# Two attention blocks on one core: K transposed in pairs of 64-row tiles on TensorE instead of partly by DMA, P transposed into score banks, Q and O copied four heads at a time

## The chip, the cores and the metric

The kernel runs on one core of one Trainium2 chip. The metric is the device time of one execution in microseconds (us). The kernel before has three timed runs: 896.97, 900.49 and 900.94 us, median 900.49. A separate, profiled execution gives the profile; its span, from the first to the last instruction, is 898.5 us.

## What is computed

Two independent blocks, A and B, of the same form; their outputs stand side by side in the last dimension.

```python
B, Sq, D, H, Sk, Dh = 16, 64, 640, 32, 512, 128      # all bfloat16
q = (x @ wq).reshape(B, Sq, H, Dh).transpose(0, 2, 1, 3)
scores = einsum("bhqd,bhkd->bhqk", q, k_cache) * (Dh ** -0.5)
p = softmax(scores, axis=-1)
o = einsum("bhqk,bhkd->bhqd", p, v_cache)
y = o.transpose(0, 2, 1, 3).reshape(B, Sq, H * Dh) @ wo
```

The keys and the values of a block are 16 x 32 x 512 x 128, 67 MB each. Four such tensors are 268 MB, by far most of what is read.

## The kernel before, in words

**Tiles.** A step is one head of a pair of batches: 2 x 64 query rows fill the 128 partitions. Two steps make a macro, m. There are 512 steps and 256 macros. Eight macros (16 heads) of one batch pair make a group, of which there are 32; eight groups, one for each batch pair, make a pass, over one half of the heads of one block. A chunk of K or V is four heads of a batch pair: two loads (one for each batch, j) of 512 KB. Two macros use one chunk of each.

**A macro's work.** Its operations have two-letter names in the code:

- KX (L457) transposes K on TensorE. K lies in `kn_ring` with the rows of two heads stacked (64 partitions each, eight rows of K in each partition). For one batch j there are eight 128x128 transposes, into one PSUM bank (7).
- KE (L466) copies that bank, 1024 elements wide, to `ktp_ring` on VectorE, and separates the two heads on the way.
- QP2 (L475) projects Q for both heads, 2 x 5 matmuls into half of bank 1. QE2 (L484) scales and copies it on ScalarE, 256 columns.
- SM (L496) forms the scores of one step as two matmuls, one for each batch, on the two column halves of the array (`tile_position`), 512 columns each. Scores have four banks, 2 to 5, used in turn.
- MX (L505, VectorE) takes the negated maximum; EX (L511, ScalarE) the exponential with the row sums; RC2 (L517, VectorE) the reciprocals of two steps; NM (L525, GpSimd) the normalised P.
- TR2 (L534) transposes P of both heads, eight 128x128 transposes into bank 6. It is copied to `pT_ring` by VectorE (TE2, L541) or by ScalarE (TA2, L546): by ScalarE for the even macros, unless the group four macros on is loaded transposed.
- PV2 (L558) multiplies with V, 16 matmuls of 64 columns into the other half of bank 1. OE2 (L566, ScalarE) copies O, 256 columns.
- OP2 (L574) adds the first 512 of 640 output columns into bank 0, over 16 heads. OX (L584) does the other 128 columns for a whole group at once, 16 matmuls into the first score bank (PSUM bank 2), in the last macro of the group. In the very last group it is split in two, so that only the last four heads' share is left for the end. The sums of the first half of the heads are kept (OVP, OXP, ScalarE); those of the second are added to them (OVF, OXF, VectorE) and stored.

**K by transposing DMA.** For 11 of the 32 groups (`TGROUPS`), K of the second batch (j = 1) does not go through KX and KE. One transposing load for each group (LDKT, L651) brings all 16 heads to `kd_sb`, from where SM reads it. Those groups have half the KX and KE.

**Order.** Nothing is scheduled at run time. `Cfg` holds a template for each engine: which operation of which macro (relative to the period) at what time of a period of two macros. The lists are unrolled over all macros; each engine works through its own in order, with semaphore waits worked out from what each operation reads and writes. A PSUM bank counts as one resource, so whoever writes a bank waits for its last reader. The loads are put into one list for SP by due times and ring slots (`SLOT_NS` and `DMA_NS` are the planner's estimates); a load into a ring waits for the last reader of the slot, and all loads behind it in the queue wait as well. Rings: four chunks of K, five of V, six slots each of wq and wo (a pass needs four of each).

Of the kernel before, what the change touches and what calls it, by code (L numbers as in the profile page):

```python
# [14 lines left out]
class Cfg:  # L15
    G = 4
    HH = 16
    NKB = 4
    NW = 6
    TGROUPS = (4, 6, 11, 13, 15, 19, 21, 23, 27, 29, 31)  # L20
    TLEAD = 1.0
    NVB = 5
    XLEAD = 1.5
    NQ = 3
    NKT = 5
# [3 lines left out]
    NO = 9  # L29
    NR = 8  # L30
    NS = 4
    PERIOD = 6.7
    PE_T = (("SM", 0, 0, 0.0), ("SM", 0, 1, 0.21), ("SM", 1, 0, 0.43), ("SM", 1, 1, 0.64), ("KX", 2, 1, 0.98),
# [3 lines left out]
    ACT_T = (("EX", 0, 0, 1.13), ("OE2", -3, 0, 2.1), ("EX", 0, 1, 2.49), ("TA2", -2, 0, 3.15), ("QE2", 3, 0, 4.0),  # L37
             ("EX", 1, 0, 4.4), ("OXP", -3, 0, 5.2), ("OE2", -2, 0, 5.34), ("EX", 1, 1, 5.73), ("OVP", -3, 0, 6.4),
             ("QE2", 4, 0, 6.65), ("ST", -3, 0, 6.68))
    DVE_T = (("MX", 0, 0, 0.44), ("MX", 0, 1, 1.06), ("RC2", -1, 0, 1.66), ("KE", 2, 1, 1.68), ("MX", 1, 0, 2.3),  # L40
             ("TE2", -2, 0, 2.6), ("RC2", 0, 0, 3.3), ("KE", 3, 1, 3.43), ("MX", 1, 1, 4.1), ("KE", 3, 0, 4.87),
             ("OXF", -3, 0, 5.3), ("OVF", -3, 0, 5.5), ("TE2", -1, 0, 5.79), ("KE", 4, 0, 6.4))
    POOL_T = (("NM", -1, 0, 1.95), ("NM", -1, 1, 2.8), ("NM", 0, 0, 4.2), ("NM", 0, 1, 5.05))
    TAIL_SPLIT = 2
    SLOT_NS = 3400.0
    DMA_NS = dict(LDK=3100.0, LDKT=9600.0, LDV=3100.0, LDWQ=3900.0, LDWO=4300.0, LDX=700.0)


class Op:
# [3 lines left out]
    def __init__(self, eng, kind, idx, reads=(), writes=(), dur=0.0, ts=None, aux=None):  # L53
        self.eng = eng
        self.kind = kind
        self.idx = idx
        self.reads = tuple(reads)
        self.writes = tuple(writes)
        self.sem = None
        self.count = None  # L60
        self.deps = []
        self.waits = []
        self.dur = dur
        self.ts = ts
        self.aux = aux
        self.dma = kind in ("LDK", "LDKT", "LDV", "LDX", "LDWQ", "LDWO", "ST")


def build_plan(dims, cfg):
# [28 lines left out]
    def by_dma(m, j=1):  # L98
        return j == 1 and m // MPG in cfg.TGROUPS

    tstart = [m for m in range(0, NMAC, MPG) if by_dma(m)]

# [3 lines left out]
    def kslot(m, j):  # L106
        return (4 * (m // 2) + (j if m % 2 == 0 else 3 - j)) % cfg.NKT

    def on_act(m):
        return m % 2 == 0 and not by_dma(min(m + 4, NMAC - 1))  # L110

    def make_op(kind, m, sub, ts):
        g0, g1 = 2 * m, 2 * m + 1
        if kind in ("KX", "KE") and by_dma(m, sub):
            return None
        ps_, bp, grp, h0 = step_info(g0)
        c = g0 // G
        if kind == "KX":
            return mk("pe", "KX", (m, sub), [("kn", c % cfg.NKB, g0 % G), ("kn", c % cfg.NKB, g1 % G), ("ident",)],
                      [("KTB",)], ts)  # L120
        if kind == "KE":
            return mk("dve", "KE", (m, sub), [], [("KTB",), ("ktp", kslot(m, sub))], ts)
# [11 lines left out]
        if kind == "QE2":  # L134
            return mk("act", "QE2", m, [], [("QOB",), ("qT", m % cfg.NQ)], ts)
        if kind == "SM":
            kt = [("ktp", kslot(m, 0)), ("kd",) if by_dma(m) else ("ktp", kslot(m, 1))]
            return mk("pe", "SM", (m, sub), [("qT", m % cfg.NQ)] + kt, [("SB", (2 * m + sub) % cfg.NS)], ts)
        if kind == "RC2":
            return mk("dve", "RC2", m, [("rowsum", r0), ("rowsum", r1)], [("recip", r0), ("recip", r1)], ts)  # L140
        if kind == "TR2":
            return mk("pe", "TR2", m, [("pn", g0 % cfg.NPN), ("pn", g1 % cfg.NPN), ("ident",)], [("PTB",)], ts)
        if kind in ("TE2", "TA2"):
            if (kind == "TA2") != on_act(m):
                return None
            return mk("dve" if kind == "TE2" else "act", kind, m, [], [("PTB",), ("pT", m % cfg.NT)], ts)
# [3 lines left out]
        if kind == "OE2":  # L150
            return mk("act", "OE2", m, [], [("QOB",), ("oT", m % cfg.NO)], ts)
        if kind == "OP2":
            return mk("pe", "OP2", m, [("oT", m % cfg.NO), ("wo", wslot(ps_, h0 // G))], [("OUTB",)], ts)
        lo = grp * MPG
        last = h0 + 2 == SPB
        if kind == "OX":
            hi = m + 1
            if grp == NGRP - 1 and h0 + 6 == SPB:
                pass
            elif not last:  # L160
                return None
            elif grp == NGRP - 1:
                lo = m - 1
            return mk("pe", "OX", m, [("oT", i % cfg.NO) for i in range(lo, hi)]
                      + [("wo", wslot(ps_, i)) for i in sorted({(2 * i % SPB) // G for i in range(lo, hi)})],
                      [("SB", 0)], ts, aux=(lo, hi))
        if not last:
            return None
        if kind in ("OVP", "OXP") and ps_ % NHALF == 0:
            return mk("act", kind, m, [], [("OUTB",) if kind == "OVP" else ("SB", 0), ("outp", bp, kind[1])], ts,  # L170
                      aux=grp)
        if kind in ("OVF", "OXF") and ps_ % NHALF == 1:
            return mk("dve", kind, m, [("outp", bp, kind[1])],
                      [("OUTB",) if kind == "OVF" else ("SB", 0), ("out_sb", kind[1])], ts, aux=grp)
# [40 lines left out]
    def tload(m):  # L215
        return at["SM", m, 0] - cfg.TLEAD

    for blk in range(NBLK):
        for lo, hi in ((0, 1), (1, 2), (2, 4), (4, NBP)) if blk == 0 else ((0, 4), (4, NBP)):
            first = at["QP2", blk * NHALF * MPP + lo * MPG, 0]  # L220
            ready = NEG if blk == 0 else at["QP2", (blk * NHALF - 1) * MPP + hi * MPG - 1, 0]
            due = [tload(m) + 0.003 for m in tstart if ready < tload(m) < first - 4]
            add(ready, due[-1] if due else first - cfg.XLEAD, first, -1, "LDX", (blk, lo),
# [10 lines left out]
    for i, m in enumerate(tstart):  # L234
        ready = NEG if i == 0 else at["SM", tstart[i - 1] + MPG - 1, 1]
        add(ready, tload(m), at["SM", m, 0], 2, "LDKT", m, [("kd",)], (m, 1), cfg.DMA_NS["LDKT"])

    for c in range(NCHUNK):
        m0 = MPC * c
        for kind, ring, n_ring, cons, tb in (("LDK", "kn", cfg.NKB, "KX", 2), ("LDV", "v", cfg.NVB, "PV2", 2.5)):  # L240
# [5 lines left out]
            for pi, (piece, j, hlo, hhi) in enumerate(chunk_pieces(c)):  # L246
                if kind == "LDK" and by_dma(m0, j):
                    continue
# [18 lines left out]
    def sem_key(op):  # L267
        if op.kind == "LDKT":
            return ("d_kd",)
# [28 lines left out]
    for op in sorted(all_ops, key=lambda o: (o.ts, ENGINES.index(o.eng))):  # L298
# [6 lines left out]
        for res in op.writes:  # L305
# [3 lines left out]
            for rd in readers.get(res, ()):  # L309
# [7 lines left out]
                NPASS=NPASS, counts=counts, KT=KT, by_dma=by_dma, wslot=wslot, kslot=kslot)  # L317
# [54 lines left out]
def mha_kernel(nc, blocks, out, cfg=None):  # L372
# [17 lines left out]
    by_dma, wslot, kslot = info["by_dma"], info["wslot"], info["kslot"]  # L390
# [14 lines left out]
    with contextlib.ExitStack() as es:  # L405
# [11 lines left out]
        kd_sb = sb("kd_sb", [128, 8, HH * 64], BF16)  # L417
        ktp_ring = sb("ktp_ring", [128, NKT, 2, SK], BF16)
        qT_ring = sb("qT_ring", [128, NQ, 2, 128], BF16)
# [3 lines left out]
        oT_ring = sb("oT_ring", [128, NO, 2, 128], BF16)  # L423
# [15 lines left out]
        pt_ps_flat = ps[:, PT_BANK, :].bitcast(BF16)  # L439
        pt_ps = pt_ps_flat.rearrange("p (s t q) -> p s t q", s=2, t=4)  # L440
        q_ps = ps[:, QO_BANK, 0:256]
        o_ps = ps[:, QO_BANK, 256:512]
        kt_ps_flat = ps[:, KT_BANK, :].bitcast(BF16)
        kt_ps = kt_ps_flat.rearrange("p (t s) -> p t s", t=8)
# [3 lines left out]

        ox_ps = ps[:, S_BANK0, 0:N1]

        def em_KX(e, op):
            m, j = op.idx
# [3 lines left out]
            for t8 in range(8):  # L456
                ins = e.transpose(kt_ps[:, t8, :], kn_ring[:, c % NKB, j, hp, t8, :], ident[:, :])  # L457
                first = first or ins
                last = ins
            return first, last  # L460

        def em_KE(e, op):
            m, j = op.idx
            src = kt_ps_flat.rearrange("p (t hs pp) -> p t hs pp", t=8, hs=2)
            dst = ktp_ring[:, kslot(m, j)].rearrange("p hs (t pp) -> p t hs pp", t=8)
            ins = e.tensor_copy(dst, src)  # L466
            return ins, ins

        def em_QP2(e, op):
            m = op.idx  # L470
            first = last = None
            for sub in range(2):
                blk, bp, grp, ps_, hh = step_info(2 * m + sub)
                for kt in range(KT):
                    ins = e.matmul(q_ps[:, sub * 128:(sub + 1) * 128],  # L475
# [6 lines left out]
        def em_QE2(e, op):  # L482
            m = op.idx
            ins = e.activation(qT_ring[:, m % NQ].rearrange("p s q -> p (s q)"), q_ps, ACTF.Copy, scale=scale)  # L484
            return ins, ins

        def em_SM(e, op):
            m, sub = op.idx
            first = last = None
            for j in range(2):  # L490
                if by_dma(m, j):
                    hh = (2 * m + sub) % SPB
                    kt = kd_sb[:, :, 64 * hh:64 * hh + 64]
                else:
                    kt = ktp_ring[:, kslot(m, j), sub, :]
                ins = e.matmul(s_bank(2 * m + sub)[64 * j:64 * j + 64, :], qT_ring[:, m % NQ, sub, 64 * j:64 * j + 64],  # L496
                               kt, start=True, stop=True, tile_position=(0, 64 * j))
# [30 lines left out]
        def em_TR2(e, op):  # L528
            m = op.idx
            first = last = None  # L530
            for sub in range(2):
                g = 2 * m + sub
                for t in range(4):
                    ins = e.transpose(pt_ps[:, sub, t, :], pn_ring[:, g % NPN, t * 128:(t + 1) * 128], ident[:, :])  # L534
# [223 lines left out]
```

## Time and profile before

| what | value |
|---|---|
| median of three runs | 900.49 us |
| the profiled execution's span | 898.5 us |
| granted TensorE clock, mean | 0.996 |
| first score matmul starts (L496) | 18.9 us |
| last K load issued (L664) | 864.8 us |
| moved by DMA | 296.81 MB, mean 330 GB/s |
| transposing loads of K (L651) | 11, of 13.5 to 15.5 us in SP's queue |
| PE waited for loads of K and V, in total | 23.2 us, of which 8.6 in one wait at the start |
| SP waited for a free K slot | 75.0 us in 79 waits |
| DVE idle, waiting for KX | 67.2 us |

The span leaves out 2.0 us of the median, what lies around it and the difference between executions; no device time of the profiled execution by itself is listed. In the profile PE is TensorE's matmuls, PEld its weight loads, DVE VectorE, ACT ScalarE, POOL GpSimd, SPq the queue that issues the loads. Lengths of matmuls on PE overlap, since they are pipelined: what one costs is read from starts, not from lengths. A line like `L457 PE MATMUL ps<-ident,kn_ring 128*128 128x128 bf16 x8` is a group of eight matmuls of code line 457, with the array's rows and columns in use, then the moving operand's shape.

### The profile page before, as it was taken

To read this page: it belongs to the slowest core of one execution; us is meant where nothing else is said; L and a number is where in the kernel's file an instruction comes from. 1 tells how busy PE (TensorE), PEld (TensorE's weight loads), DVE (VectorE), ACT (ScalarE), POOL (GpSimd) and SP (SyncE) were. 2 spreads that over 40 slices of the span, in tenths; PEclk is the share of its full clock that TensorE was granted. 3 is DMA by queue.
4 is the path that set the end of the run, shared out by engine and by line. 5 is a ranking of instruction groups with operands and counts; after the bars stand their busy time and mean duration, and the time that the engine had idled before them with its cause. 6 is when DMAs were issued, how large, how long until landed. Compare 5 with 4: busy or idle time off the path is not lost.

```text
span 898.5 us, 33204 instructions
## 1 busy us (share of the span) xinstructions
PE 857.5 (95%) x14016; PEld 691.1 (77%) x14144; DVE 746.6 (83%) x1398; ACT 628.0 (70%) x1651; POOL 413.8 (46%) x518
## 2 busy tenths in 40 slices
PE   4999989999999999999998998999999999999997
PEld 3777777878888877878786787778778777787875
DVE  2888878888888888888887887888888798888896
ACT  1776766777777777767676776777777676776774
POOL 0544444445444454544444444445454444545453
PEclk9999999999999999999999999999999999999999
DMA  9999999999999999999999999999999999999992
GB/s 304 336 340 365 318 272 365 295 361 365 363 366 368 286 361 322 319 369 270 364 361 368 367 260 365 309 324 366 294 363 363 367 370 284 367 286 365 315 333 77
DMA packets 315172, 296.81 MB, mean 330 GB/s; under 512 B 109200, under 2 KB 260752, under 8 KB 315024
## 3 DMA queue, kind: packets, MB, share of 16 engines
q1 hardware_dynamic: 312720, 292.06, 106.3%
q10 hardware_dynamic: 2304, 2.62, 0.9%
q8 instruction: 111, 1.82, 0.9%
q14 instruction: 37, 0.30, 0.1%
HBM read 266.34 MB, written 2.62 MB: 299 GB/s over the span
## 4 chain that ended last, share of the span: by engine, by line
PE 78%; DMA 9%; SPq 7%; DVE 3%; issue 1%; ACT 1%; DVEq 0%; ACTq 0%
PE ps L457 20%; PE ps L475 14%; PE ps L496 12%; PE ps L558 11%; PE ps L534 10%; PE ps L574 9%; DMA kn_ring<-in_B_k_cache_dram 5%; DMA kn_ring<-in_A_k_cache_dram 4%; SPq L651 3%; PE ps L584 3%; SPq L644 2%; DVE ktp_ring L466 1%; SPq L664 1%; DMA wq_sb<-in_A_wq_dram 1%; DVE negmax L505 1%
## 5 line engine op out<-in xcount | busy, mean ns | idle before, releaser
L525 POOL TENSOR_SCALAR pn_ring<-p_ring,recip 128x512 bf16<-128x512 bf16 x512 | 413.1, 843 | 476.1 <-DVE recip L517 475.7
L511 ACT ACTIVATE p_ring<-ps,negmax 128x512 bf16<-128x512 f32 x512 | 350.1, 684 | 100.0 <-DVE negmax L505 100.0
L466 DVE COPY ktp_ring<-ps 128x1024 bf16<-128x1024 bf16 x424 | 290.0, 684 | 82.1 <-PE ps L457 67.2
L505 DVE TENSOR_REDUCE negmax<-ps 128x1 f32<-128x512 f32 x512 | 337.3, 680 | 15.2 <-PE ps L496 4.9
L457 PEld LDWEIGHTS ps<-ident,kn_ring 128*128 128x128 bf16 x3392 | 205.3, 98 | 108.5 <-issue 46.5
L457 PE MATMUL ps<-ident,kn_ring 128*128 128x128 bf16 x3392 | 263.6, 221 | 21.1 <-DMA kn_ring<-in_A_k_cache_dram 11.8
L475 PE MATMUL ps<-xT_sb,wq_sb 128*128 128x128 bf16 x2560 | 187.8, 221 | 1.3 <-DMA wq_sb<-in_A_wq_dram 0.6
L558 PE MATMUL ps<-pT_ring,v_ring 128*128 128x64 bf16 x4096 | 162.0, 193 | 8.6 <-DMA v_ring<-in_B_v_cache_dram 3.1
L475 PEld LDWEIGHTS ps<-xT_sb,wq_sb 128*128 128x128 bf16 x2560 | 154.4, 99 | 16.9 <-ACT oT_ring L566 15.8
L558 PEld LDWEIGHTS ps<-pT_ring,v_ring 128*128 128x128 bf16 x4096 | 141.9, 98 | 28.5 <-issue 26.5
L484 ACT ACTIVATE qT_ring<-ps 128x256 bf16<-128x256 f32 x256 | 98.3, 384 | 86.1 <-PE ps L475 86.0
L534 PE MATMUL ps<-ident,pn_ring 128*128 128x128 bf16 x2048 | 156.4, 219 | 0.0
L566 ACT ACTIVATE oT_ring<-ps 128x256 bf16<-128x256 f32 x256 | 97.6, 381 | 75.3 <-PE ps L558 68.1
L541 DVE COPY pT_ring<-ps 128x1024 bf16<-128x1024 bf16 x174 | 119.5, 687 | 35.5 <-PE ps L534 35.5
L496 PE MATMUL ps<-ktp_ring,qT_ring 128*64 128x512 bf16 x848 | 137.3, 391 | 0.0
L574 PE MATMUL ps<-wo_sb,oT_ring 128*128 128x512 bf16 x384 | 124.5, 379 | 6.8
L534 PEld LDWEIGHTS ps<-ident,pn_ring 128*128 128x128 bf16 x2048 | 118.5, 98 | 0.0
L511 ACT ACTIVATION_READ_ACCUMULATOR p_ring<-ps,negmax 128x1 f32 x512 | 103.1, 201 | 0.0
L546 ACT ACTIVATE pT_ring<-ps 128x1024 bf16<-128x1024 bf16 x82 | 84.0, 1024 | 0.0
L496 PEld LDWEIGHTS ps<-ktp_ring,qT_ring 128*64 128x64 bf16 x848 | 47.1, 110 | 41.0 <-issue 2.1
L517 DVE RECIPROCAL recip<-rowsum 128x2 f32<-128x2 f32 x256 | 40.9, 160 | 14.7 <-ACT p_ring L511 14.6
L496 PE MATMUL ps<-kd_sb,qT_ring 128*64 128x512 bf16 x176 | 47.0, 390 | 0.0
(15 smaller groups left out, 152.0 us busy)
## 6 DMA issues: line engine op xcount, KB each, us to landing
v_ring<-in_A_v_cache_dram SPq DMA_DIRECT2D x128, 512.0 KB, 9.9
v_ring<-in_B_v_cache_dram SPq DMA_DIRECT2D x126, 512.0 KB, 9.8
kn_ring<-in_A_k_cache_dram SPq DMA_DIRECT2D x108, 512.0 KB, 9.4
kn_ring<-in_B_k_cache_dram SPq DMA_DIRECT2D x103, 512.0 KB, 9.3
wq_sb<-in_A_wq_dram SPq DMA_DIRECT2D x8, 640.0 KB, 9.9
wo_sb<-in_A_wo_dram SPq DMA_DIRECT2D x8, 640.0 KB, 10.7
wq_sb<-in_B_wq_dram SPq DMA_DIRECT2D x8, 640.0 KB, 9.7
wo_sb<-in_B_wo_dram SPq DMA_DIRECT2D x8, 640.0 KB, 10.3
```

Source lines behind the costliest of these rows:

```text
L457: ins = e.transpose(kt_ps[:, t8, :], kn_ring[:, c % NKB, j, hp, t8, :], ident[:, :])
L466: ins = e.tensor_copy(dst, src)
L475: ins = e.matmul(q_ps[:, sub * 128:(sub + 1) * 128], wq_sb[:, wslot(ps_, hh // G), kt, (hh % G) * DH:(hh % G + 1) * DH], xT_sb[:, kt, bp * ...
L484: ins = e.activation(qT_ring[:, m % NQ].rearrange("p s q -> p (s q)"), q_ps, ACTF.Copy, scale=scale)
L496: ins = e.matmul(s_bank(2 * m + sub)[64 * j:64 * j + 64, :], qT_ring[:, m % NQ, sub, 64 * j:64 * j + 64], kt, start=True, stop=True, tile_ ...
L505: ins = e.reduce_max(negmax[:, r:r + 1], s_bank(g), axis=AX.X, negate=True)
L511: ins = e.activation(p_ring[:, g % NP, :], s_bank(g), ACTF.Exp, bias=negmax[:, r:r + 1], scale=1.0, accum_out=rowsum[:, r:r + 1])
L525: ins = e.tensor_scalar(dst, src, recip[:, r:r + 1], 1.0, ALU.mult, ALU.mult)
L534: ins = e.transpose(pt_ps[:, sub, t, :], pn_ring[:, g % NPN, t * 128:(t + 1) * 128], ident[:, :])
L541: ins = e.tensor_copy(pT_ring[:, m % NT].rearrange("p s t q -> p (s t q)"), pt_ps_flat)
L558: ins = e.matmul(o_ps[:, col:col + 64], v_ring[:, c % NVB, j, gi, t, :], pT_ring[:, m % NT, sub, t, 64 * j:64 * j + 64], start=(t == 0), s ...
L574: ins = e.matmul(out_ps, oT_ring[:, m % NO, sub, :], wo_sb[:, wslot(ps_, hh // G), hh % G, 0:N0], start=(hh == 0), stop=(hh == SPB - 1))
```

## The change

- **KX** now handles a whole macro: both batches, 32 transposes instead of 2 x 8. Each takes 64 rows (one head) and an identity of 64 columns. The first 64 rows go to bank 6, the other 64 to bank 7, in turn. KE copies both banks at once, 2048 elements, without rearranging. `ktp_ring` has two slots, each of a macro, in place of five of half a macro.
- **No K by transposing DMA**: `TGROUPS`, LDKT and `kd_sb` are gone, and all of K comes by plain loads. The ring of K has five chunks and that of V six.
- **TR2** writes P into the first of the four score banks for even macros and into the second for odd ones; ScalarE copies the even ones, VectorE the odd ones. **OX** uses the third of the four, and is no longer split in the last group.
- **Q and O**: the two macros of a period write Q of four heads into the whole of bank 1, which QE4 copies at once (512 columns); then O of four heads, which OE4 copies at once.
- New templates for all engines, with PV2 one macro earlier (offsets -2 and -1 in place of -3 and -2), and new planner estimates.

```diff
-    NKB = 4
+    NKB = 5
-    TGROUPS = (4, 6, 11, 13, 15, 19, 21, 23, 27, 29, 31)
-    NVB = 5
+    NVB = 6
-    NQ = 3
-    NKT = 5
+    NQ = 2
+    NKT = 2
-    NO = 9
+    NO = 5
-    PERIOD = 6.7
-    PE_T = (("SM", 0, 0, 0.0), ("SM", 0, 1, 0.21), ("SM", 1, 0, 0.43), ("SM", 1, 1, 0.64), ("KX", 2, 1, 0.98),
-            ("PV2", -3, 0, 1.43), ("TR2", -2, 0, 1.9), ("OP2", -4, 0, 2.35), ("KX", 3, 1, 2.78), ("QP2", 3, 0, 3.23),
-            ("OP2", -3, 0, 3.79), ("OX", -3, 0, 4.2), ("KX", 3, 0, 4.22), ("PV2", -2, 0, 4.67), ("TR2", -1, 0, 5.14),
-            ("KX", 4, 0, 5.59), ("QP2", 4, 0, 6.04))
+    PERIOD = 6.3
+    PE_T = (("SM", 0, 0, 0.0), ("SM", 0, 1, 0.21), ("SM", 1, 0, 0.43), ("SM", 1, 1, 0.64), ("KX", 2, 0, 0.95),
+             ("QP2", 2, 0, 2.17), ("TR2", -2, 0, 2.27), ("QP2", 3, 0, 3.1), ("TR2", -1, 0, 3.44), ("KX", 3, 0, 3.48),
+             ("OP2", -4, 0, 4.05), ("PV2", -2, 0, 4.32), ("OP2", -3, 0, 4.57), ("OX", -3, 0, 4.7),
+             ("PV2", -1, 0, 5.62))
+    ACT_T = (("OE4", -4, 0, 0.41), ("EX", 0, 0, 1.51), ("EX", 0, 1, 2.49), ("TA2", -2, 0, 3.76), ("QE4", 2, 0, 4.13),
+             ("EX", 1, 0, 4.21), ("EX", 1, 1, 4.98), ("OVP", -3, 0, 5.82), ("OXP", -3, 0, 6.03), ("ST", -3, 0, 6.25))
+    DVE_T = (("RC2", -1, 0, 0.51), ("MX", 0, 0, 0.79), ("MX", 0, 1, 1.66), ("KE", 2, 0, 1.84), ("MX", 1, 0, 2.57),
+             ("MX", 1, 1, 3.68), ("RC2", 0, 0, 3.77), ("TE2", -1, 0, 5.1), ("KE", 3, 0, 5.14), ("OVF", -3, 0, 5.42),
+             ("OXF", -3, 0, 5.87))
+    POOL_T = (("NM", -1, 1, 2.95), ("NM", -1, 0, 3.28), ("NM", 0, 1, 4.1), ("NM", 0, 0, 5.62))
+    ACT_TE = (0,)
+    TRB = (0, 1)
+    OXB = 2
...
-        S_BANK0 = 2
-        OUT_BANK, QO_BANK, PT_BANK, KT_BANK = 0, 1, 6, 7
+        OUT_BANK, QO_BANK, S_BANK0, KT_BANK0 = 0, 1, 2, 6
...
+        def pt_flat(m):
+            return s_bank(cfg.TRB[m % 2]).bitcast(BF16)
...
-            for t8 in range(8):
-                ins = e.transpose(kt_ps[:, t8, :], kn_ring[:, c % NKB, j, hp, t8, :], ident[:, :])
+            for j in range(2):
+                for t8 in range(8):
+                    for hs in range(2):
+                        r = slice(64 * hs, 64 * hs + 64)
+                        ins = e.transpose(kt_ps[hs][:, j, 64 * t8:64 * t8 + 64], kn_ring[r, c % NKB, j, hp, t8, :],
+                                          ident[r, 64 * hs:64 * hs + 64])
...
-            src = kt_ps_flat.rearrange("p (t hs pp) -> p t hs pp", t=8, hs=2)
-            dst = ktp_ring[:, kslot(m, j)].rearrange("p hs (t pp) -> p t hs pp", t=8)
-            ins = e.tensor_copy(dst, src)
+            ins = e.tensor_copy(ktp_ring[:, op.idx % NKT].rearrange("p hs j s -> p (hs j s)"), kt_all)
...
-            ins = e.activation(qT_ring[:, m % NQ].rearrange("p s q -> p (s q)"), q_ps, ACTF.Copy, scale=scale)
+            ins = e.activation(qT_ring[:, op.idx % NQ].rearrange("p s q -> p (s q)"), qo_ps, ACTF.Copy, scale=scale)
...
-            ins = e.activation(oT_ring[:, m % NO].rearrange("p s q -> p (s q)"), o_ps, ACTF.Copy)
+            ins = e.activation(oT_ring[:, op.idx % NO].rearrange("p s q -> p (s q)"), qo_ps, ACTF.Copy)
```

More of the change, by code (lines that the diff above doesn't have):

```diff
@@ L96, in mk, with trbank @@
         return Op(eng, kind, idx, reads, writes, dur=dur, aux=aux, ts=ts)
-    def by_dma(m, j=1):
-        return j == 1 and m // MPG in cfg.TGROUPS
-    tstart = [m for m in range(0, NMAC, MPG) if by_dma(m)]
     def wslot(ps_, j):
         return (ps_ * HG + j) % cfg.NW
[L106 to L110, printed above, removed]
+    def trbank(m):
+        return cfg.TRB[m % 2]
     def make_op(kind, m, sub, ts):
         g0, g1 = 2 * m, 2 * m + 1
-        if kind in ("KX", "KE") and by_dma(m, sub):
-            return None
         ps_, bp, grp, h0 = step_info(g0)
         c = g0 // G
+        k = m // 2
         if kind == "KX":
-            return mk("pe", "KX", (m, sub), [("kn", c % cfg.NKB, g0 % G), ("kn", c % cfg.NKB, g1 % G), ("ident",)],
+            return mk("pe", "KX", m, [("kn", c % cfg.NKB, g0 % G), ("kn", c % cfg.NKB, g1 % G), ("ident",)],
                       [("KTB",)], ts)
         if kind == "KE":
-            return mk("dve", "KE", (m, sub), [], [("KTB",), ("ktp", kslot(m, sub))], ts)
+            return mk("dve", "KE", m, [], [("KTB",), ("ktp", m % cfg.NKT)], ts)
         if kind in ("MX", "EX", "NM"):
@@ L149, in make_op @@
                       [("QOB",)], ts)
-        if kind == "OE2":
-            return mk("act", "OE2", m, [], [("QOB",), ("oT", m % cfg.NO)], ts)
+        if kind == "OE4":
+            return mk("act", "OE4", k, [], [("QOB",), ("oT", k % cfg.NO)], ts)
         if kind == "OP2":
-            return mk("pe", "OP2", m, [("oT", m % cfg.NO), ("wo", wslot(ps_, h0 // G))], [("OUTB",)], ts)
+            return mk("pe", "OP2", m, [("oT", k % cfg.NO), ("wo", wslot(ps_, h0 // G))], [("OUTB",)], ts)
+        if h0 + 2 != SPB:
+            return None
         lo = grp * MPG
-        last = h0 + 2 == SPB
         if kind == "OX":
[L157 to L168, printed above, removed]
+            return mk("pe", "OX", m, [("oT", i % cfg.NO) for i in range(lo // 2, k + 1)]
+                      + [("wo", wslot(ps_, i)) for i in range(HG)], [("SB", cfg.OXB)], ts, aux=(lo, m + 1))
         if kind in ("OVP", "OXP") and ps_ % NHALF == 0:
-            return mk("act", kind, m, [], [("OUTB",) if kind == "OVP" else ("SB", 0), ("outp", bp, kind[1])], ts,
+            return mk("act", kind, m, [], [("OUTB",) if kind == "OVP" else ("SB", cfg.OXB), ("outp", bp, kind[1])], ts,
                       aux=grp)
@@ L221, in build_plan @@
             ready = NEG if blk == 0 else at["QP2", (blk * NHALF - 1) * MPP + hi * MPG - 1, 0]
-            due = [tload(m) + 0.003 for m in tstart if ready < tload(m) < first - 4]
-            add(ready, due[-1] if due else first - cfg.XLEAD, first, -1, "LDX", (blk, lo),
+            add(ready, first - cfg.XLEAD, first, -1, "LDX", (blk, lo),
                 [("xT", bp) for bp in range(lo, hi)], (blk, lo, hi), cfg.DMA_NS["LDX"] * (hi - lo))
@@ L416, in mha_kernel @@
         v_ring = sb("v_ring", [128, NVB, 2, G, 4, DH], BF16)
-        kd_sb = sb("kd_sb", [128, 8, HH * 64], BF16)
-        ktp_ring = sb("ktp_ring", [128, NKT, 2, SK], BF16)
-        qT_ring = sb("qT_ring", [128, NQ, 2, 128], BF16)
+        ktp_ring = sb("ktp_ring", [128, NKT, 2, 2, SK], BF16)
+        qT_ring = sb("qT_ring", [128, NQ, 4, 128], BF16)
         p_ring = sb("p_ring", [128, NP, SK], BF16)
@@ L490, in em_SM @@
             for j in range(2):
[L491 to L497, printed above, removed]
+                ins = e.matmul(s_bank(2 * m + sub)[64 * j:64 * j + 64, :],
+                               qT_ring[:, m // 2 % NQ, 2 * (m % 2) + sub, 64 * j:64 * j + 64],
+                               ktp_ring[:, m % NKT, sub, j, :], start=True, stop=True, tile_position=(0, 64 * j))
                 first = first or ins
@@ L533, in em_TR2 @@
                 for t in range(4):
-                    ins = e.transpose(pt_ps[:, sub, t, :], pn_ring[:, g % NPN, t * 128:(t + 1) * 128], ident[:, :])
+                    ins = e.transpose(pt_flat(m)[:, (4 * sub + t) * 128:(4 * sub + t + 1) * 128], pn_ring[:, g % NPN, t * 128:(t + 1) * 128], ident[:, :])
                     first = first or ins
@@ L583, in em_OX @@
                 blk, bp, grp, ps_, hh = step_info(g)
-                ins = e.matmul(ox_ps, oT_ring[:, g // 2 % NO, g % 2, :], wo_sb[:, wslot(ps_, hh // G), hh % G, N0:DN],
+                ins = e.matmul(ox_ps, oT_ring[:, g // 4 % NO, g % 4, :], wo_sb[:, wslot(ps_, hh // G), hh % G, N0:DN],
                                start=(hh == 0), stop=(hh == SPB - 1))
```

95 lines of the change are left out of this document (34 added, 61 removed).

## The prediction, made before the changed kernel was run

> **What bounds the kernel now.** I read the share of busy time first, then the slices, then one steady period of TensorE in order of time, then the stretches of 10 or 20 us.
>
> ```profile
> PE 857.5 (95%) x14016; PEld 691.1 (77%) x14144; DVE 746.6 (83%) x1398; ACT 628.0 (70%) x1651; POOL 413.8 (46%) x518
> ...
> GB/s 304 336 340 365 318 272 365 295 361 365 363 366 368 286 361 322 319 369 270 364 361 368 367 260 365 309 324 366 294 363 363 367 370 284 367 286 365 315 333 77
> ...
> PE 78%; DMA 9%; SPq 7%; DVE 3%; issue 1%; ACT 1%; DVEq 0%; ACTq 0%
> ```
>
> The chain that ended last lies on PE for 78%. The GB/s row has a ceiling of 365 to 370 and dips to 260 to 295. Whether the ceiling is saturation is told by the stretches (busy times of PE, PEld, DVE, ACT, POOL; clock; DMA share; GB/s):
>
> ```profile
> 0.00:10.00 10.00, 1.01 (x8) 0.78 (x8) 0.37 (x1) 1.28 (x1) 0.68 (x6) 1.00 0.74 225
> 380.00:400.00 20.00, 19.72 (x332) 15.78 (x333) 17.28 (x35) 13.97 (x39) 10.88 (x14) 1.00 1.08 367
> 400.00:420.00 20.00, 19.80 (x335) 16.36 (x335) 17.43 (x34) 14.18 (x38) 8.39 (x12) 1.00 1.16 272
> 870.00:880.00 10.00, 9.95 (x175) 7.91 (x173) 8.53 (x17) 5.78 (x18) 4.27 (x6) 1.00 1.10 353
> 880.00:890.00 10.00, 8.71 (x143) 6.16 (x143) 7.96 (x17) 7.62 (x22) 7.34 (x10) 1.00 0.06 18
> ```
>
> The DMA share is above 1 up to 880 us: the engines are never idle, and 367 GB/s is what they give. In 400 to 420 us one transposing load of K (issued at 401.7) takes them down to 272. So **two resources are full together**: TensorE, and the transfers until 880, after which 18.5 us of work remain. To gain, a change must shorten both.
>
> One period (two macros) on TensorE, start and length:
>
> ```profile
> 401.81 1.05 PE L496 MATMUL ps<-ktp_ring,qT_ring 128*64 128x512 bf16 x8
> 402.80 0.62 PE L457 MATMUL ps<-ident,kn_ring 128*128 128x128 bf16 x8
> 403.26 0.63 PE L558 MATMUL ps<-pT_ring,v_ring 128*128 128x64 bf16 x16
> 403.73 0.61 PE L534 MATMUL ps<-ident,pn_ring 128*128 128x128 bf16 x8
> 404.39 0.38 PE L574 MATMUL ps<-wo_sb,oT_ring 128*128 128x512 bf16 x1
> 404.60 0.61 PE L457 MATMUL ps<-ident,kn_ring 128*128 128x128 bf16 x8
> 405.05 0.72 PE L475 MATMUL ps<-xT_sb,wq_sb 128*128 128x128 bf16 x10
> 405.61 0.59 PE L574 MATMUL ps<-wo_sb,oT_ring 128*128 128x512 bf16 x2
> 406.04 0.61 PE L457 MATMUL ps<-ident,kn_ring 128*128 128x128 bf16 x8
> 406.49 0.63 PE L558 MATMUL ps<-pT_ring,v_ring 128*128 128x64 bf16 x16
> 406.95 0.61 PE L534 MATMUL ps<-ident,pn_ring 128*128 128x128 bf16 x8
> 407.44 0.62 PE L457 MATMUL ps<-ident,kn_ring 128*128 128x128 bf16 x8
> 407.89 0.72 PE L475 MATMUL ps<-xT_sb,wq_sb 128*128 128x128 bf16 x10
> 408.54 0.41 PE L496 MATMUL ps<-ktp_ring,qT_ring 128*64 128x512 bf16 x2
> ```
>
> Read the starts, since the lengths overlap. No gap is left: 6.73 us from scores to scores, of which the four K transposes take 4 x 0.45 = 1.80. Sixteen matmuls of 64 columns take 403.26 to 403.73: **29 ns each**; eight transposes of 128 columns take 0.45: 56 each.
>
> And two narrow views, of the matmuls and of the weight loads:
>
> ```profile
> 401.81 0.41 PE L496 MATMUL ps<-ktp_ring,qT_ring 128*64 128x512 bf16 x2
> ```
> ```profile
> 402.80 0.11 PEld L457 LDWEIGHTS ps<-ident,kn_ring 128*128 128x128 bf16 x2 [0.41 <-issue]
> ```
>
> Two score matmuls on the two column halves of the array end 0.41 us after the first began, though one lasts 0.40 by the row's maximum of 404 ns: halves run side by side. Two full-width weight loads of 98 ns fit into 0.11, so a load may follow a load by some 12 ns.
>
> **The change, part by part.**
>
> *K transposes.* Per macro, 16 transposes of 128 columns (2 x 0.45 = 0.90 us) become 32 of 64 rows by 64 columns, ordered as 16 pairs on the two row halves. No row of this trace shows row halves. Nearest rows: 64 columns in 29 ns, halves side by side, loads 12 ns apart. If a pair takes 29 ns, a macro's take 16 x 29 = 0.46; if the members follow each other, 32 x 29 = 0.93. I take 0.46, because the score row shows pairs of halves overlapping wholly and two loads (24 ns) fit into 29; 0.93 is the other end. Nothing points below 0.46, since 29 ns for 64 columns has the same ns per column as 56 for 128.
>
> *Changing the array's form.* Into the scores TensorE loses 0.09 us (408.54 less 407.89 less 10 x 56 ns), out of them 0.12 (402.80 less 401.81 less 4 x 0.216). I take 0.10 for each change. Before there are two per period; after, five: into the scores, scores to K, K to Q, P transposes to K, K to the output projection. Three more cost 0.30; the ends are 0 and 0.36. The Trainium skill, "TensorEngine Tiling (Array Packing)", section "Tiling Modes", says that changing the mode drains TensorE; the 0.09 and 0.12 agree for column halves, and by that rule the three changes are not free.
>
> *Period.* 6.73 - 1.80 + 2 x 0.46 + 0.30 = 6.15. Every fourth period has the 16 small output matmuls L584, 0.89 us (412.77 to 413.66), so the mean is 6.37.
>
> *The groups loaded transposed* (11 of 32) had only two K transposes per period, 5.84 us; they become 6.15, slower by 0.31, and are in the mean.
>
> *VectorE.* KE copies 2048 elements in place of 1024. A copy of 1024 lasts 684 ns and takes 0.59 from start to start (403.54 to 404.13); doubled elements add some 0.53 (684 less the 0.15 of the two-element reciprocal), so 1.12. Per period: four maxima at 0.61, two KE at 1.12, one P copy 0.61, two reciprocals at 0.08, finals 0.1: 5.55 of 6.15. It hides, with 0.6 to spare; without that cover each 0.1 us costs 13 us over 128 periods.
>
> *ScalarE.* Two copies of 256 columns (384 and 381 ns) become one of 512; the copy of 512 at L592 takes 596. From start to start a 256-column copy takes 0.28, so one of 512 takes 0.28 + 0.21 = 0.49; two of these, four exponentials at 0.66 and one P copy at 0.94 are 4.6 of 6.15. Hidden.
>
> *Added waits.* (1) The P transposes go into the first two score banks, so they wait for the exponential of that bank. Exponential 0 starts 1.24 us after the scores (403.05) and ends at 1.93; the P transpose comes after scores 0.99, K 0.46, change 0.10, Q 0.56 = 2.11: 0.18 to spare. Behind it queue the second Q, the second P transpose, K and everything else on PE. (2) Q and O share a bank as before, but now all four heads: the first PV waits for QE4. P copy from 2.76, QE4 from 3.70 to 4.30; PE gets there at 4.64. Behind it: output projection, second PV. (3) The second KX waits for the first KE (1.67 to about 2.9); PE arrives at 3.65. All are covered; the first is the thinnest. GpSimd's two normalisations (0.84 each) end over 1 us ahead of the P transposes.
>
> *DMA.* The same bytes; the 11 transposing loads go, and with them the dips. 296.8 MB at 366 GB/s are 811 us, plus 3.9 lost in the first 10 us (225 GB/s), some 5 around the six x transposes (331 and 343 GB/s in 20 to 40 and 40 to 60 us for the first four, 3.2 us, and half that for the other two), and 18.5 after the last: 838. Instructions took 1.82 MB for 33,204; 9,600 more are 0.5 MB, 1.4 us: 840. SP issues 22 plain loads more for 11 transposing ones of 14.3 us each, which held its queue longer. Five K and six V chunks in place of four and five cost nothing.
>
> *Sum.* First scores start at 18.9 us, last period at 883.6, 14.9 from the end. 18.9 + 127 x 6.37 + 14.9 = 842.8; the last group's small output matmuls are no longer split, 12 x 56 ns = 0.7. So 843.5 by PE, 840 by DMA. Two limits this close don't overlap perfectly: after the start PE waited 14 us for loads before, at the same balance. I take 9.5. **Span 853**; the median of the runs, 900.5, is 2.0 above the span of 898.5, so **855 us**.
>
> **The rivals.**
>
> *A: the transposes follow each other (slower).* If a macro's 32 take 0.93 us, the period is 7.08, the mean 7.30: 18.9 + 927 + 14.9 + 0.7 + 2 = 964. If the chip treats 64 rows simply as a smaller transpose (the change doesn't do what it says), the three changes of form go too: 6.78, mean 7.00: 926. It decides from 40 ns per pair: 11 ns more than 29, times 32, is 0.35 us, 45 us in all. For it: no row halves in this trace, and no sustained stream below 29 ns. Against: the score pairs. Beside it stands the Trainium skill, "TensorE: Matmul & The Clock Gate", section "Wait — 56ns, not 53.3ns?": starts never come closer than about 25 ns however few the columns. The score pair, two ends within 0.01, speaks against its holding across halves; if it holds, an estimate is 50 ns per pair, 7.04 mean, 931.
>
> *B: transfers set the pace.* Weights are 8 x 0.655 MB per pass, 14.3 us of DMA, four times; if the chunks held ahead absorb only half, 28 us appear as waits: 846 + 28 = 874. For it: saturation. Against: 40 us less DMA work than now.
>
> *C: a new wait.* If the P transposes come 0.2 us late each period: 855 + 26 = 881.
>
> **How the numbers follow.** Forecast 0.62 (838 to 868), B 0.10, C 0.05, A 0.20, offsetting parts near zero 0.03. A measurement tells about 0.5% (4.5 us) from no change: faster 0.77, same 0.03, slower 0.20. The range leaves out A and little else: 838 to 905.
>
> **What would show it.** Pairs in which both transposes start within a few ns and the next pair 29 ns on; K blocks of 0.46 us; scores to scores 6.15 and 7.04; DMA flat at 365; no PE wait on L511's exponential. It is wrong if the K block takes 0.6 us or more, or if PE waits for loads exceed 20 us.

## The result, and the profile after

The changed kernel takes **973.4 us** (median; 964.4 to 979.1) against 900.3 for the kernel before: a ratio of 1.079, 95% interval 1.074 to 1.084. The prediction was 855, range 838 to 905, so it was wrong, and on the wrong side. (One disturbed execution is left out of the ratio.) The profiled execution took 972.0, with a span of 970.3 us.

The page after: busy time, GB/s in 40 slices, the queue that brings instructions (packets, MB, share), and the chain by engine.

```profile
PE 830.5 (86%) x18817; PEld 657.9 (68%) x18944; DVE 727.6 (75%) x1184; ACT 642.0 (66%) x1441; POOL 416.4 (43%) x518
...
GB/s 306 321 346 365 317 366 350 284 319 327 317 283 370 368 315 279 302 294 269 354 252 350 367 323 313 306 292 295 295 343 192 368 369 333 321 276 322 311 164 16
...
q8 instruction: 149, 2.44, 1.0%
...
PE 81%; issue 12%; SPq 4%; DMA 2%; DVE 0%; POOL 0%; ACT 0%; POOLq 0%; ACTq 0%
```

PE is busy for less time than before (830 us after 857), and yet the span is longer: TensorE stands still. The chain names no culprit but "issue", 12% of the span, 116 us: time in which PE waited for nothing that the profile shows. The dips in GB/s are still there without the transposing loads. The queue q8 brought 149 packets of instructions; before, the same row of the page was

```profile
q8 instruction: 111, 1.82, 0.9%
```

149 packets of 256 instructions are 38,144, and TensorE's own stream after the change has 18,944 weight loads, as many matmuls and some 390 waits: q8 brings TensorE's instructions.

One period on TensorE, in order of time:

```profile
400.26 0.60 PE L539 MATMUL ps<-wo_sb,oT_ring 128*128 128x512 bf16 x2
400.69 0.28 PE L524 MATMUL ps<-pT_ring,v_ring 128*128 128x64 bf16 x4
402.39 0.52 PE L524 MATMUL ps<-pT_ring,v_ring 128*128 128x64 bf16 x12 [1.42 <-issue]
402.84 1.05 PE L461 MATMUL ps<-ktp_ring,qT_ring 128*64 128x512 bf16 x8
403.83 0.64 PE L429 MATMUL ps<-ident,kn_ring 64*128 64x64 bf16 x32
404.40 0.73 PE L446 MATMUL ps<-xT_sb,wq_sb 128*128 128x128 bf16 x10
...
407.53 0.28 PE L524 MATMUL ps<-pT_ring,v_ring 128*128 128x64 bf16 x4
409.76 0.51 PE L524 MATMUL ps<-pT_ring,v_ring 128*128 128x64 bf16 x12 [1.95 <-issue]
```

Two things are to be seen. The disputed block is as fast as forecast: 32 transposes and one change of form from 403.83 to 404.40, 0.57 us. And PE stops **in the middle of a block**: four of 16 PV matmuls, 1.4 us of nothing, then the other twelve. Matmuls 5 to 16 of that block wait for no semaphore of their own; their data were there for the first four. What can still be missing is the instructions themselves. The DMA view says when those came. Of the stretches 399.9 to 401.0, 401.0 to 402.4, 402.4 to 407.3 and 407.3 to 408.6 us only the first and the last have a row of the instruction queue:

```profile
q8 instruction: 1, 0.02, 5.3%
```

That is one packet of 16 KB. In the trace's records the two packets land at 400.95 and 408.52, and PE goes on at 402.39 and 409.76, 1.44 and 1.24 us later. Over the whole trace, 87 stops, 115 us in all, end 1.1 to 1.75 us after a packet of instructions landed, most of them 1.2 to 1.6, and they stand **256 instructions apart** in TensorE's stream: 16 KB at 64 bytes each. (A line through their positions has a slope of 255.1 here, where 127 matmul records are missing, and 256.0 in the traces of the runs below that miss none.) Before there were 4 such stops, 4 us.

The Trainium skill, "Runtime: NRT & Kernel Launch", section "Instruction fetch mechanics", says that an engine's instructions come in blocks of 16 KiB, 256 instructions, through a DMA queue of its own while the block before is executed, and that the cost is mostly hidden. The blocks of 256 agree with the trace; "mostly hidden" doesn't hold here, by the 115 us.

What SP waited for tells what became of the loads. Line, waits in us, times, longest:

```profile
SPq L622 <- PE ps L429: 342.2, 97, 9.9
```

It waited 342 us for a free K slot, where it was 75 before: TensorE frees the slots late, so the loads are held up by it, not the reverse. Not all of the rise comes from the stops: in a run below that has 2 us of them, SP still waited 221 us.

### The profile page after: what moved, and what is told of

Read it like the earlier page. It is cut to its first block, busy times and chain, and to the rows that moved or that the text cites. A ratio compares the mean times of both kernels' runs of the same rounds, so it can differ in the third digit from the quotient of the medians.

```text
span 970.3 us, 42285 instructions
## 1 busy us (share of the span) xinstructions
PE 830.5 (86%) x18817; PEld 657.9 (68%) x18944; DVE 727.6 (75%) x1184; ACT 642.0 (66%) x1441; POOL 416.4 (43%) x518
## 4 chain that ended last, share of the span: by engine, by line
PE 81%; issue 12%; SPq 4%; DMA 2%; DVE 0%; POOL 0%; ACT 0%; POOLq 0%; ACTq 0%
PE ps L446 16%; PE ps L429 15%; PE ps L461 13%; PE ps L524 12%; PE ps L500 11%; PE ps L539 10%; PE ps L549 3%; DMA v_ring<-in_A_v_cache_dram 2%; SPq L622 1%; SPq L618 1%; SPq L609 1%; SPq L595 0%; DVE negmax L471 0%; SPq L603 0%; POOL pn_ring L491 0%
## 5 line engine op out<-in xcount | busy, mean ns | idle before, releaser
L436 DVE COPY ktp_ring<-ps 128x2048 bf16<-128x2048 bf16 x256 | 312.5, 1221 | 64.0 <-PE ps L429 63.5
L429 PEld LDWEIGHTS ps<-ident,kn_ring 64*128 64x128 bf16 x8192 | 138.9, 96 | 124.3 <-issue 108.9
L429 PE MATMUL ps<-ident,kn_ring 64*128 64x64 bf16 x8192 | 174.2, 192 | 50.6 <-issue 41.9
L524 PEld LDWEIGHTS ps<-pT_ring,v_ring 128*128 128x128 bf16 x4096 | 155.9, 99 | 84.0 <-issue 33.1
L531 ACT ACTIVATE oT_ring<-ps 128x512 bf16<-128x512 f32 x128 | 76.4, 597 | 165.6 <-PE ps L524 165.6
L512 ACT ACTIVATE pT_ring<-ps 128x1024 bf16<-128x1024 bf16 x128 | 130.9, 1023 | 54.4 <-PE ps L500 47.4
L507 DVE COPY pT_ring<-ps 128x1024 bf16<-128x1024 bf16 x128 | 86.3, 675 | 14.7 <-PE ps L500 14.7
L454 ACT ACTIVATE qT_ring<-ps 128x512 bf16<-128x512 f32 x128 | 75.8, 592 | 13.5 <-PE ps L446 13.4
L549 PEld LDWEIGHTS ps<-wo_sb,oT_ring 128*128 128x128 bf16 x512 | 31.4, 98 | 18.4 <-issue 11.1
L549 PE MATMUL ps<-wo_sb,oT_ring 128*128 128x128 bf16 x512 | 34.8, 219 | 9.8 <-issue 9.8
```

Source lines behind the costliest of these rows:

```text
L429: ins = e.transpose(kt_ps[hs][:, j, 64 * t8:64 * t8 + 64], kn_ring[r, c % NKB, j, hp, t8, :], ident[r, 64 * hs:64 * hs + 64])
L436: ins = e.tensor_copy(ktp_ring[:, op.idx % NKT].rearrange("p hs j s -> p (hs j s)"), kt_all)
L512: ins = e.activation(pT_ring[:, m % NT].rearrange("p s t q -> p (s t q)"), pt_flat(m), ACTF.Copy)
L524: ins = e.matmul(qo_ps[:, col:col + 64], v_ring[:, c % NVB, j, gi, t, :], pT_ring[:, m % NT, sub, t, 64 * j:64 * j + 64], start=(t == 0), ...
L549: ins = e.matmul(ox_ps, oT_ring[:, g // 4 % NO, g % 4, :], wo_sb[:, wslot(ps_, hh // G), hh % G, N0:DN], start=(hh == 0), stop=(hh == SPB ...
```

## The experiments

**Theories.** Q: the packet with TensorE's next instructions stands in the DMA engines behind the loads of K and V, and comes too late when 256 instructions are executed faster than a packet is fetched. F: a fetch takes its 6.5 us (the median distance of two packets in the changed kernel) whatever else is loaded. S: the stops are waits of the new order that the profile can't name. For each block I took the time from the moment the block before it is begun (inferred from the positions of the stops) to the start of its packet: the *delay*. In the changed kernel its median is 3.9 us; the packet then takes 1.1, and 1.4 pass until PE goes on: 6.4. Executing 256 instructions takes 5.2 to 5.4 there.

### Loads in flight: two or three, three or four, five or six

```diff
-        def run_program(e, prog, final_waits=()):
-            for op in prog:
+        def run_program(e, prog, final_waits=(), depth=0):
+            for i, op in enumerate(prog):
+                if depth and i >= depth:
+                    landed = prog[i - depth]
+                    if landed.count == max(o.count for o in prog[:i] if o.sem == landed.sem):
+                        e.wait_ge(sems[landed.sem], landed.count * 16)
...
-            run_program(sync, progs["sp"])
+            run_program(sync, progs["sp"], depth=2)
```

(depth 3 and 5 in the others.)

> The changed kernel, with one addition: SP waits for earlier loads to land, so that only two or three loads of 512 KB are in flight (before it: six or so, by 8 to 9 us from issue to landing). Theory Q: TensorE stands still because the fetch of its next 16 KB of instructions (256 of them) lies in the DMA engines behind the loads; with a short backlog the fetch comes in time. Expected: the 115 us of stops tied to fetches fall below 25, the period is 6.15 / 7.04 nearly everywhere, the time 850 to 880. Rival F: a fetch takes its 6.5 us whatever is loaded; time unchanged, 960 to 985. Rival S: the stops are waits of the new order (score banks, the bank of Q and O) that the profile can't name; time unchanged or slower.

> As the run before, with three or four loads in flight. Theory Q: a longer backlog than with two or three, so some stops come back: 855 to 910, not faster than with two or three unless the loads themselves starve there. Rivals F and S: 960 to 985.

> The changed kernel with five or six loads in flight (three or four gave 958.9 us: stops at fetches 11 us instead of 115, but TensorE waited for loads instead; two or three 1229.5). Theory Q: between the two: fewer stops at fetches than 115 us and nearly the full rate of loads: 925 to 965. If 5 or 6 are as many as the queue holds anyway: 970.

Measured: 1229.5, 958.9 and 963.1 us (ratios to the kernel before 1.368, 1.062 and 1.071, intervals 1.363 to 1.374, 1.054 to 1.071 and 1.065 to 1.078). The first two forecasts of Q fail as times: the loads starve. The moved bytes of the runs with two or three and with three or four loads in flight, and the chain of the first:

```profile
DMA packets 236724, 297.38 MB, mean 243 GB/s; under 512 B 19456, under 2 KB 171008, under 8 KB 236544
...
DMA 97%; SPq 1%; issue 1%; PE 1%; DVE 0%; POOL 0%; POOLq 0%; ACT 0%
```
```profile
DMA packets 236725, 297.39 MB, mean 309 GB/s; under 512 B 19456, under 2 KB 171008, under 8 KB 236544
...
GB/s 245 289 282 314 308 315 323 303 313 337 311 292 325 312 325 336 306 311 308 308 300 311 315 317 309 312 329 316 321 313 309 307 319 324 343 333 341 322 318 152
```

But the stops at fetches fell from 115 us to 11 with three or four (its trace is of an execution of 963.1 us), and the delay from 3.9 to 2.4 us (1.7 with two or three). The fewer stops alone prove little, since TensorE waits for loads here and needs its instructions later. The delay says more: blocks whose packet came while loads ran at 365 GB/s or more had a median delay of 2.3 to 2.6 there, by the stretch over which the rate is taken, and of 4.0 in the changed kernel. At the same rate, a shorter backlog lets the packet through sooner. That speaks for Q, against F and S. With five or six the fetches are as without a limit: delay 3.9, stops 109 us. As a remedy it fails: with three or four in flight no slice of the run passes 343 GB/s, where the changed kernel's best reach 370, so what shortens the backlog enough also costs the rate.

### Fewer bytes, the same instructions

```diff
-                ins = e.dma_start(v_ring[:, c % NVB, j, hlo:hhi], src)
+                if c >= NVB:
+                    mid = (hlo + hhi) // 2
+                    ins = e.dma_start(v_ring[:, c % NVB, j, hlo:mid], src[:, 0:mid - hlo])
+                else:
+                    ins = e.dma_start(v_ring[:, c % NVB, j, hlo:hhi], src)
```

(The second run loads one head of V, `hlo:hlo + 1`, and likewise one of two pairs of K.) Both leave out loads that the result needs and compute with what lies in the rings, so they are experiments and no remedy.

> The changed kernel, with work left out: after the first six chunks, V is loaded for only two of the four heads of a chunk (the other two are taken from what an earlier chunk left there). TensorE executes the same instructions in the same order; 67 MB less are loaded, so the DMA engines are no longer full. Theory Q: the stops tied to fetches nearly vanish, time 846 to 860 (the sum by PE of the prediction). Rival F: 960 to 985, since the number of instructions is the same. Rival S: 960 to 985, since all waits between engines are the same.

> The changed kernel with more work left out: once the rings have been filled, of each chunk only one of four heads of V and two of four of K are loaded. TensorE's instructions are the same as in the changed kernel. Theory Q (a fetch of instructions waits behind loads): with some 130 MB instead of 297 the engines are mostly free, the fetch starts within 1 to 1.5 us of the moment it is wanted and nearly all stops go: 846 to 865. Theory F (256 instructions cannot come faster than one block per 6.5 us): 960 or more. In the run with V halved, stops stood where loads ran at over 330 GB/s and not where they ran below 250; so F would have to fail here too.

Measured: 911.6 (ratio 1.014, 1.008 to 1.021) and **859.5 us** (0.956, 0.951 to 0.961). With V halved, Q's time failed: 63 us of stops were left, since the loads still come in bursts at the full rate. Rows of that run (busy times, clock, DMA share, GB/s):

```profile
480.00:500.00 20.00, 18.95 (x438) 14.57 (x436) 16.61 (x28) 15.07 (x34) 10.24 (x13) 1.00 1.03 348
500.00:520.00 20.00, 16.82 (x378) 13.23 (x374) 14.27 (x23) 13.15 (x30) 7.52 (x10) 1.00 0.88 298
520.00:540.00 20.00, 20.00 (x483) 15.82 (x481) 17.16 (x30) 16.22 (x38) 9.82 (x12) 1.00 0.81 240
```

PE gets through 438, 378 and then, at 240 GB/s, 483 matmuls in 20 us. Over the whole run, of the 32 blocks whose packet had to pass loads of 365 GB/s or more 19 stopped TensorE (median delay 3.9 us), and of the 35 below 250 GB/s only 3 (1.2 us). The instructions are the same, so F and S fall. With the light loads:

```profile
300.00:400.00 100.00, 100.00 (x2320) 78.58 (x2313) 89.92 (x149) 76.43 (x174) 52.37 (x64) 1.00 0.43 133
```

PE has no gap in 100 us; the delay is 0.56 us, stops are 16 us, mostly in the first periods and where weights are loaded. The period is 6.15 us and 7.04 in nearly all of the run, **as the prediction had it**, and 859.5 lies 14 above its sum of 843.5 + 2.

### Fewer instructions, and idle ones in their place

```diff
-            for j in range(2):
-                for t8 in range(8):
-                    for hs in range(2):
-                        r = slice(64 * hs, 64 * hs + 64)
-                        ins = e.transpose(kt_ps[hs][:, j, 64 * t8:64 * t8 + 64], kn_ring[r, c % NKB, j, hp, t8, :],
-                                          ident[r, 64 * hs:64 * hs + 64])
+            for j in range(2):
+                for t8 in range(8):
+                    ins = e.transpose(kt_w[j][:, 128 * t8:128 * t8 + 128], kn_ring[:, c % NKB, j, hp, t8, :], ident[:, :])
```

and for the second run, in addition:

```diff
                 first, last = emitters[op.kind](e, op)
+                if op.eng == "pe":
+                    for _ in range(4):
+                        e.wait_ge(sems[("s_init",)], 2)
```

> The changed kernel with one part undone: K is transposed by 128x128 transposes again (16 for a macro, two heads each, one bank for each batch) in place of 32 of 64 rows; KE separates the heads in its copy. Everything else (no K by DMA, P into score banks, Q and O of four heads) stays. TensorE has 64 instructions less per period of about 298. By the sum: period 6.15 - 0.92 - 0.30 + 1.80 = 6.73, with the small output matmuls 6.95 on average, 919 us in all. Theory Q (and F): 234 instructions per 6.95 us need a 16 KB block every 7.6 us, as in the kernel before, so few stops: 915 to 940, faster than the changed kernel. Rival S: the stops stay, 1000 or more.

> The changed kernel with 128x128 K transposes (912.6 us), and four waits more after each of TensorE's 15 operations of a period, on a semaphore that has long reached its value: 60 instructions of 64 bytes more per period, no work for the array and no real wait, so that the number of instructions is that of the changed kernel. Theory Q: stops tied to fetches come back, as far as the loads fill the DMA engines: 955 to 1010. If the row tiles or the shape of their transposes were the cause and not the number of instructions: 912 to 925. What the waits cost in TensorE's sequencer by themselves isn't known from a trace; if the time grows without stops at fetches, it is that.

Measured: 912.6 us (ratio 1.016, 1.011 to 1.020) and 947.7 (1.054, 1.047 to 1.061). The first lies a little below the 915 to 940 of Q. With 128x128 transposes PE does more work and the kernel is 61 us faster than the changed one:

```profile
PE 889.9 (98%) x14848; PEld 740.0 (81%) x14848; DVE 728.8 (80%) x1184; ACT 641.4 (70%) x1441; POOL 416.2 (46%) x518
...
span 910.9 us, 34220 instructions
...
GB/s 307 339 341 366 336 369 367 367 361 359 337 284 370 370 368 321 320 299 315 363 291 369 367 327 365 358 319 310 322 364 252 366 368 369 349 309 308 332 116 16
...
q8 instruction: 117, 1.92, 0.9%
...
PE 92%; SPq 5%; DMA 2%; DVE 0%; POOL 0%; issue 0%; POOLq 0%; ACT 0%
```

"issue" is gone from the chain, and stops at fetches are 2 us. Idle waits, with the same work for the array, bring them back:

```profile
span 948.7 us, 37869 instructions
...
q8 instruction: 132, 2.16, 0.9%
...
PE 91%; SPq 4%; issue 3%; DMA 2%; DVE 0%; POOL 0%; POOLq 0%; ACT 0%
```

The edit asks for sixty waits per period, but the program has only 3,649 instructions more, some 28 per period: in the trace most of the added instructions carry two waits each. So the number of instructions comes about halfway to that of the changed kernel, not up to it as the expectation says: 132 packets, between 117 and 149. The usual period stays at 6.68 us in both, so the waits themselves cost no time; 46 stops at fetches, 29 us, do, and smaller ones. The 947.7 lies somewhat under the 955 to 1010 that I gave, which were for the full number; a block of 256 lasts 6.7 us there, near the time of a fetch. The kernel has no row tiles at all, so it is the number of instructions, not the row tiles.

### How many pairs fit

```diff
+        def pairs(m):
+            return m % 2 == 0
```

with pairs of 64-row tiles where this holds and 128x128 transposes elsewhere; `m % 4 == 0` in the second run.

> The changed kernel with pairs of 64-row tiles for even macros only and 128x128 transposes for odd ones: 266 instructions per period, halfway. By the sum of the parts: period 6.73 - 0.44 + 0.10 = 6.39, with the small output matmuls 6.61, 876 us without stops. Theory Q: a block of 256 per 6.15 us where a fetch takes 6.4 under full loads, so stops of a quarter of a us per block at most and only in the stretches of full loads: 878 to 905. This is the version that could beat both. Rival S: stops in proportion to pairs, 930 to 950.

> The changed kernel with pairs of 64-row tiles for every fourth macro only and 128x128 transposes for the rest. With pairs for all, half and none of the macros the shortest periods were 6.15, 6.36 and 6.68 us and the stops tied to fetches 115, 28 and 2 us. Theory Q: here 250 instructions per period, on average 6.52 (6.74 with the small output matmuls), 892 us without stops, and 3 to 12 us of stops, since a block of 256 lasts 6.7 us where a fetch under full loads takes 6.4: 893 to 905, no more than level with the kernel before. If stops go with the number of pairs and have no threshold (115 us times a quarter): 915 to 925.

Measured: 902.0 us (ratio 1.004, 1.002 to 1.006) and **894.2 us** (0.993, 0.991 to 0.995), the only complete version here that beats the kernel before, by 0.7%. Both lie in the ranges that Q gave. Side by side, with the whole change and with none of its pairs:

| macros with pairs | packets of instructions | shortest period, us | stops at fetches, us | median, us |
|---|---|---|---|---|
| all | 149 | 6.15 | 115 | 973.4 |
| every 2nd | 133 | 6.36 | 28 | 902.0 |
| every 4th | 125 | 6.36 and 6.68 in turn | 3 | 894.2 |
| none | 117 | 6.68 | 2 | 912.6 |

The stops don't go with the number of pairs: half of the pairs leave a quarter of them, a quarter of the pairs next to none. With every second macro 256 instructions last 6.3 us, just less than the 6.4 of a fetch; with every fourth most blocks last longer. The 6.4 is a median and no sharp line: with the idle waits above, blocks of 6.7 us still had 46 stops. That run has nearly as many packets as the one with every second macro, 132 against 133, and nearly the same stops, 29 us against 28, by waits alone.

### No K by transposing DMA, alone

```diff
-    TGROUPS = (4, 6, 11, 13, 15, 19, 21, 23, 27, 29, 31)
+    TGROUPS = ()
```

> The kernel before with one part of the change alone: no K by transposing DMA; all of K goes through 128x128 transposes on TensorE (the buffer for the transposed loads is left unused, the rings stay at four and five chunks). By the page: all 32 groups then take 27.8 us, 6.73 us a period and 7.62 with the small output matmuls, 18.9 + 127 x 6.95 + 15 + 2 = 919; the transfers have no dips any more. If it comes near the changed kernel with 128x128 transposes (912.6), then P in the score banks and the copies of four heads neither gain nor cost more than a few us, and the whole loss of the change lies in the pairs; if it is 930 or more, those parts gain.

Measured: 923.9 us (ratio 1.026, 1.024 to 1.028), between the two marks of the expectation: this part alone costs 23 us, since every group now takes 27.81 us. The changed kernel with 128x128 transposes is 11 us below it (9 by the two ratios). So P in the score banks, the wider copies, the larger rings and the new order together gain some 10 us by themselves: 0.047 per period, 6 us, and first scores at 15.0 instead of 19.4, 4 us.

## Why the prediction was wrong, point by point

- *A pair takes 29 ns, a macro's K transposes 0.46 us.* Right. A narrow view of TensorE shows 16 of them in 0.41 us including the length of the last:

```profile
403.83 0.41 PE L429 MATMUL ps<-ident,kn_ring 64*128 64x64 bf16 x16
```

  One lasts 0.19, so 15 starts follow the first within 0.22 us: under 15 ns each, two in the 29 of a pair. In the trace's records the two of a pair start 2 to 3 ns apart, and the next pair 29 ns on. The rule of the Trainium skill that the prediction set beside rival A ("TensorE: Matmul & The Clock Gate", section "Wait — 56ns, not 53.3ns?", no starts closer than about 25 ns) doesn't hold across row halves. Rival A's mechanism was wrong; that its 964 lies near the result is chance.
- *Each change of form costs 0.10.* Right: by the trace's starts 0.093 to 0.096 each, at all five.
- *Period 6.15, and 7.04 with the small output matmuls.* Right: the shortest periods of the changed kernel are 6.150 and 7.043.
- *VectorE and ScalarE hide.* Right: KE 1221 ns, Q and O copies 592 and 597.
- *The added waits are covered.* Right: PE waited 1.7 us in all for an exponential ahead of a P transpose.
- *Transfers: flat at 365 GB/s, 840 us.* Wrong in the result, as a consequence: TensorE held the loads up, and they ran at 306 on average. The prediction also laid the dips to the transposing loads alone. The run with 128x128 transposes has none of these and 2 us of stops, and its slices still go down to 252 GB/s, with SP waiting 221 us for free K slots.
- **The step that failed** is in the sum of the transfers: "9,600 more are 0.5 MB, 1.4 us". I counted instructions as bytes. The size was near (q8 brought 0.62 MB more); the deadline was missing. Instructions are a stream with a deadline: one block of 256 has to come before the block ahead of it is done. Before, 111 packets in 898 us, one in 7.5 us (the median distance), against 6.4 for a fetch under full loads: covered. After, one is due every 5.4 us (the median in the run with light loads). The stops, 115 us, make the difference of 843.5 to 970.3 but for 12 us. The remainder was not taken apart. The start (the third period takes 12.1 us) and shorter stops belong to it, and so does the granted clock: 0.984 on the mean, 0.996 before, since for 31 us of this execution it was at half, with eight transposes of P in 0.85 us instead of 0.45. TensorE stood idle for a third of those 31 us, so an estimate is up to 10 us.
- *9.5 us for two limits this close together.* The third limit, fetching instructions, stood as close as these two, and it was the one that the change moved the wrong way.

**What stays open.** Where a packet of instructions waits, in the queues of the DMA engines or on the way to memory, was not separated; that the delay falls with the backlog at the same rate points to the queues. When TensorE asks for a packet isn't in the trace; the delay is counted from an inferred moment.

## What to carry to other kernels

Count an engine's instructions per microsecond as a resource of their own. The page gives it: packets of the instruction queue over the span. If loads fill the DMA engines, many small matmuls that are cheap for the array can cost more than fewer large ones, and a stop in the middle of a block without a semaphore, put down to "issue", is how it looks. Then use the cheap form only as far as its instructions can be fetched: here one macro in four.

## What the runs showed of the hardware that was not expected

- TensorE executed 256 instructions in 5.2 to 5.4 us; fetching the next 256 took 6.4 at the median in the changed kernel, with loads of 306 GB/s on the mean and up to 370 (delay 3.9, packet 1.1, 1.4 until the first matmul), and 3.1 under light ones (delay 0.56).
- Transposes in 64-row halves run side by side: two 64-column transposes in 29 ns, the time of one.
- Loads of 512 KB needed more than three or four in flight for the full rate: 243 GB/s on the mean with two or three, and no slice above 343 with three or four, against 365 to 370 in the best slices without a limit.
- Idle waits on TensorE, some 28 instructions per period of 6.68 us, cost no time except by being fetched.
